# Where a decode kernel turns a group's V sums: behind the first chunk of the next K pair, or behind its first half

## The chip, the cores and the metric

One core of a Trainium2 chip. The metric is device time in microseconds of one execution. The kernel before took 1346.06 us (median of three runs, 1346.02 to 1346.26). All runs below are of state fast, and every verdict compares a kernel with the kernel before, run on the same chip in the same rounds.

## The reference

Two branches are mixed. Branch A, which takes nearly all the time, is attention for one decoded token over a cache: batch 4, 32 heads, 8192 keys of 128 elements, in bf16.

```python
q = (x @ wq).reshape(B, Sq, H, Dh).transpose(0, 2, 1, 3)
scores = jnp.einsum("bhqd,bhkd->bhqk", q, k_cache) * (Dh ** -0.5)
p = _softmax(scores, axis=-1)
o = jnp.einsum("bhqk,bhkd->bhqd", p, v_cache)
a = o.transpose(0, 2, 1, 3).reshape(B, Sq, H * Dh) @ wo
...
return g * a + (1 - g) * b      # b: a gated MLP on the same token, g: a sigmoid gate
```

The K cache and the V cache are 268 MB each and each byte is used once. So the core has to bring in about 0.58 GB whatever it computes.

## The kernel before

K and V come in "pairs" of two ring slots, 4.2 MB a slot, for four heads. The ring has 5 slots (NS) and all loads go out in program order on one queue, that of SP. A load waits until the slots that it writes are free.

```python
    def load_pair(src, n, apart=False):
        a = slots(2)
        if a + 1 < NS and not apart:
            lo = a * RING
            nc.sync.dma_start(out=flat[:, lo:lo + 2 * n], in_=src)     # one load into two slots
            return [flat[:, lo:lo + n], flat[:, lo + n:lo + 2 * n]]
        halves = [ring[:, a], ring[:, (a + 1) % NS]]                   # or one load for each slot
        ...
```

A K pair is worked off in 8 chunks (RD), four (JT) in each slot. DVE transposes a chunk into T, of which there are two buffers, and PE multiplies T with the spread-out query.

```python
    def k_pair(d):
        ...
        ks = load_pair(kv_view(A_k_cache, d), RING)
        for n in range(RD):
            kn, c = ks[n // JT], n % JT
            T = ttp.tile([P, CJ, 2, 32, 2], BF, name="T", tag="T")
            nc.vector.transpose(out=T[:]..., in_=kn[:, c * CJ * Dh:(c + 1) * CJ * Dh]...)       # L370
            ...
            for he in range(4):
                ...
                for z in range(2):
                    nc.tensor.matmul(sps[:, z, :], lhsT=Z[:, he, s:s + P], rhs=T[...], ...)    # L376
            if n == 0:
                flush()
            if n == 2:
                flush_late()
        if t == GD - 1:
            softmax(g)
```

Four pairs make a group. V pairs follow the K pairs at a distance of a group. When a group's last V pair is done, ACT and DVE gather its sums into OS; what then remains to be done (PE turns the sums so that the 128 elements of a head lie along the partitions, and DVE scales them) is only noted down, and `flush()` and `flush_late()` emit it at a later place in PE's and DVE's programs:

```python
        def finish():
            oT = small([P, GH])
            for q in range(4):                                   # the "turning": fp32, four matmuls
                nc.tensor.matmul(oT[:, :], lhsT=o_sb[:, q * Dh:(q + 1) * Dh],                   # L466
                                 rhs=selg[:, q].rearrange("p t s -> p (t s)"), start=(q == 0), stop=(q == 3))

            def scaled():                                        # the scaling, on DVE
                ...
                nc.vector.scalar_tensor_tensor(out=OT[:, hg:hg + GH, b], in0=oT[:, :], ...)     # L471
            late.append(scaled)
        pending.append(finish)
```

The order is K pair d, V pair d - 4, K pair d + 1, and so on. Of eight groups, six are turned in a K pair (pairs 8, 12, 16, 20, 24 and 28), one in a V pair and one at the end of the program.

Of the kernel before, what the change touches and what calls it, by code (L numbers as in the profile page):

```python
# [56 lines left out]
def kernel(  # L57
# [25 lines left out]
    JT = JR // CJ  # L83
# [38 lines left out]
# [5 lines that stand above are left out]
            nc.sync.dma_start(out=flat[:, lo:lo + 2 * n], in_=src)  # L127
            return [flat[:, lo:lo + n], flat[:, lo + n:lo + 2 * n]]
        halves = [ring[:, a], ring[:, (a + 1) % NS]]
        for i, half in enumerate(halves):  # L130
            nc.sync.dma_start(out=half[:, 0:n], in_=src[:, i * n:(i + 1) * n])
        return halves
# [202 lines left out]
    def flush():  # L335
        while pending:
            pending.pop(0)()

    def flush_late():
        while late:  # L340
            late.pop(0)()
# [4 lines left out]
    def kv_view(cache, d):  # L346
        b, h0 = heads(d)
        return cache[b, h0:h0 + NQ].rearrange("h (r j) d -> (h r) (j d)", j=2 * JR)

    def spread(d):  # L350
        b, h0 = heads(d)
        Z = Zt[d % 2]
        nc.gpsimd.tensor_tensor(out=Z[:, :, QP - 1:QP - 1 + P].rearrange("p e (q c) -> p e q c", c=QP)[:, :, :, 0],  # L353
                                in0=qa[:, :, h0:h0 + NQ, b], in1=mq[:].to_broadcast([P, 4, NQ]), op=ALU.mult)

    def k_pair(d):
        g, t = divmod(d, GD)
        Z = Zt[d % 2]
        if d == 0:
            spread(0)  # L360
        if d + 1 < ND:
            spread(d + 1)
        if t == 0:
            S_ps[g] = scp.tile([P, 2, 512], F32, name="S_ps")
        sps = S_ps[g]
# [4 lines that stand above are left out]
            nc.vector.transpose(out=T[:].rearrange("p j h i e -> p (j h i e)").bitcast(U32),  # L370
                                in_=kn[:, c * CJ * Dh:(c + 1) * CJ * Dh].bitcast(U32))
            s = QP - 1 - (RD * t + n)
            for he in range(4):
                half, e = divmod(he, 2)
                for z in range(2):
                    nc.tensor.matmul(sps[:, z, :], lhsT=Z[:, he, s:s + P], rhs=T[:, 16 * z:16 * z + 16, half, :, e],  # L376
                                     start=(t == 0 and n == 0 and he == 0),
                                     stop=(t == GD - 1 and n == RD - 1 and he == 3))
            if n == 0:
                flush()  # L380
            if n == 2:
                flush_late()
        if t == GD - 1:
            softmax(g)
# [102 lines left out]
    for kind, d in order:  # L487
        if kind == "k":
            k_pair(d)
            if d in side:  # L490
                side[d]()
        if (kind, d) == ("v", ND - 1):
            for g in range(2):
                wo_block(g)()
        if kind == "v":
            v_pair(d)
        if (kind, d) == ("k", ND // 2):
            add_x()
        if (kind, d) == ("v", ND - 2):
            o_rows(0, GE)  # L500
# [44 lines left out]
```

## Time and profile before

| what | before |
|---|---|
| time, median of 3 | 1346.06 us |
| moved by the loads | 576.2 MB, 429 GB/s over the span |
| the load queue's share of 16 DMA engines | 99.5% |
| PE busy, DVE busy | 78%, 46% |
| K and V loads in one piece, issue to landing (medians) | 33.3 and 29.8 us |

These are lines of the page of the kernel before: busy time by engine; the share of DMA busy and GB/s in 40 equal slices of the span; the load queue; and the chain of waits that ended last.

```profile
span 1343.2 us, 7989 instructions
...
PE 1050.1 (78%) x4536; PEld 230.3 (17%) x2348; DVE 617.8 (46%) x358; ACT 51.4 (4%) x46; POOL 58.7 (4%) x91
...
DMA  9999999999999999999999999999999999999998
GB/s 414 440 427 431 436 430 425 446 427 424 440 430 427 440 433 422 442 434 428 436 434 433 424 431 436 434 434 439 418 424 437 434 429 434 432 429 442 422 425 335
...
q1 hardware_dynamic: 14132, 575.69, 99.5%
...
DMA 62%; PE 20%; DVE 11%; issue 6%; another core or an unknown queue 0%; DVEq 0%; ACT 0%; SPq 0%
DMA ring<-in_A_k_cache_dram 52%; PE S_ps L376 11%; DVE T L370 11%; PE o_ps L447 8%; DMA ring<-in_A_v_cache_dram 7%; DMA ring<-in_B_w_gate_dram 3%; DMA ring<-in_A_wo_dram 1%; PE small L466 1%; DVEq L370 0%; PE acc L212 0%; ACT OS L459 0%; ACT res L513 0%; SPq L142 0%; SPq L144 0%
```

The digits 9 and the 99.5% say that the DMA engines hardly rest. Packets of one engine can overlap (a share in the windows below reaches 1.10), so the share alone is a sign of it and no proof. The chain needs care. It gives PE 20% and DVE 11%, which looks as if a third of the span were the engines'. But a load of the chain begins with its issue, not with its first byte, so the piece "DVE T" or "PE S_ps" between two loads only says what the second load's issue waited for. Whether that issue was late is not in the chain.

The first K pair of a group, at 482.8 us, shows the place that the change is about. First DVE's timeline (start, duration, instruction, count, and in brackets the idle time before it with what ended it). The eight transpositions of K pair 12 stand in three rows; the scaling L471 is behind the third chunk, and the last row is the next K pair's first one.

```profile
482.83 4.51 DVE L370 STREAM_TRANSPOSE T<-ring 128x2048 uint32<-128x2048 uint32 x2 [2.39 <-DMA ring<-in_A_k_cache_dram]
488.90 2.31 DVE L370 STREAM_TRANSPOSE T<-ring 128x2048 uint32<-128x2048 uint32 x1 [1.56 <-PE S_ps L376]
491.13 0.21 DVE L471 SCALAR_TENSOR_TENSOR OT<-small,sgb,rinv 128x16 bf16<-128x16 f32 x1
493.83 11.09 DVE L370 STREAM_TRANSPOSE T<-ring 128x2048 uint32<-128x2048 uint32 x5 [2.48 <-PE S_ps L376]
521.72 2.31 DVE L370 STREAM_TRANSPOSE T<-ring 128x2048 uint32<-128x2048 uint32 x1 [16.80 <-DMA ring<-in_A_k_cache_dram]
```

DVE rests 1.56 us before chunk 2 and 2.48 us before chunk 3. Both are waits for a T buffer: chunk 2 needs the one that PE's chunk 0 reads, chunk 3 the one that PE's chunk 1 reads. PE's timeline of the same stretch:

```profile
485.29 3.57 PE L376 MATMUL S_ps<-T,Z 128*128 128x512 bf16 x8 [6.36 <-DVE T L370]
488.66 1.72 PE L466 MATMUL small<-selg,OS 128*128 128x16 f32 x8
490.22 5.36 PE L376 MATMUL S_ps<-T,Z 128*128 128x512 bf16 x16
496.20 1.90 PE L376 MATMUL S_ps<-T,Z 128*128 128x512 bf16 x8 [0.62 <-DVE T L370]
```

Chunk 0 (8 matmuls) takes 3.57 us, the turning (8 records, since each fp32 matmul is two) 1.72 us, and then the next 16 matmuls 5.36 us, although a chunk at full speed takes 1.90 us. The columns are busy time with counts for PE, PE's weight loads, DVE, ACT and POOL, then the granted clock, the DMA share and GB/s.

```profile
core 0: us, PE busy (x) PEld busy (x) DVE busy (x) ACT busy (x) POOL busy (x), PEclk, DMA share, GB/s
485.30:488.60 3.30, 3.30 (x8) 0.83 (x5) 2.04 (x1) 0.00 (x0) 0.00 (x0) 0.50 1.10 477
488.60:490.20 1.60, 1.60 (x9) 1.54 (x8) 1.30 (x1) 0.00 (x0) 0.00 (x0) 0.50 0.95 410
490.20:493.50 3.30, 3.30 (x9) 0.68 (x6) 1.15 (x2) 0.00 (x0) 0.00 (x0) 0.50 1.01 437
493.50:497.00 3.50, 2.88 (x13) 0.58 (x6) 3.17 (x2) 0.00 (x0) 0.00 (x0) 0.96 0.91 393
```

PE had waited for the load and started at half clock, and the clock came back only after chunk 1, at about 493.8 us. So what stands between chunk 0 and chunk 1 runs at half speed.

When chunk 3 is done, the first slot is free and SP issues the next K load. SP's timeline:

```profile
472.06 0.33 SPq L127 DMA_DIRECT2D ring<-in_A_v_cache_dram  x1
496.17 0.33 SPq L127 DMA_DIRECT2D ring<-in_A_k_cache_dram  x1
```

### The profile page before, as it was taken

Reading aid. Unit: us, or ns where it says so; the run is one execution under the profiler, and the core shown is the slowest. Engines: PE = TensorE matmul, PEld = TensorE weight load, DVE = VectorE, ACT = ScalarE, POOL = GpSimd, SP = SyncE. Lnnn points to the kernel's source line nnn. Section 1 sums busy time; section 2 is a strip of 40 time slices with the busy share of each in tenths; the row PEclk is TensorE's granted clock in tenths of the full one; section 3 lists DMA queues with packets and bytes.
Section 4 is the critical chain, followed back from the end, with each engine's and each line's share of the span. In section 5 each row is a group of like instructions: output and inputs, shape, how many; then the busy total and the mean of one; then the engine's idle time right before and its main releaser. Section 6 shows DMA issues by size and latency. Waiting matters only on the chain.

```text
span 1343.2 us, 7989 instructions
## 1 busy us (share of the span) xinstructions
PE 1050.1 (78%) x4536; PEld 230.3 (17%) x2348; DVE 617.8 (46%) x358; ACT 51.4 (4%) x46; POOL 58.7 (4%) x91
## 2 busy tenths in 40 slices
PE   2565877788797778778987789797789679877898
PEld 0111111111111111111211121111111112111221
DVE  2455655535445554335455446246555254556000
ACT  0000100001000100001000010001000010000000
POOL 4000100001000100001000010000000010000000
PEclk9777988978998989899888889998899799989899
DMA  9999999999999999999999999999999999999998
GB/s 414 440 427 431 436 430 425 446 427 424 440 430 427 440 433 422 442 434 428 436 434 433 424 431 436 434 434 439 418 424 437 434 429 434 432 429 442 422 425 335
DMA packets 14175, 576.20 MB, mean 429 GB/s; under 512 B 1582, under 2 KB 1590, under 8 KB 2108
## 3 DMA queue, kind: packets, MB, share of 16 engines
q1 hardware_dynamic: 14132, 575.69, 99.5%
q8 instruction: 27, 0.44, 0.1%
q14 instruction: 8, 0.07, 0.0%
q10 hardware_dynamic: 8, 0.00, 0.0%
HBM read 575.68 MB, written 0.01 MB: 429 GB/s over the span
## 4 chain that ended last, share of the span: by engine, by line
DMA 62%; PE 20%; DVE 11%; issue 6%; another core or an unknown queue 0%; DVEq 0%; ACT 0%; SPq 0%
DMA ring<-in_A_k_cache_dram 52%; PE S_ps L376 11%; DVE T L370 11%; PE o_ps L447 8%; DMA ring<-in_A_v_cache_dram 7%; DMA ring<-in_B_w_gate_dram 3%; DMA ring<-in_A_wo_dram 1%; PE small L466 1%; DVEq L370 0%; PE acc L212 0%; ACT OS L459 0%; ACT res L513 0%; SPq L142 0%; SPq L144 0%
## 5 line engine op out<-in xcount | busy, mean ns | idle before, releaser
L370 DVE STREAM_TRANSPOSE T<-ring 128x2048 uint32<-128x2048 uint32 x256 | 570.8, 2282 | 498.5 <-DMA ring<-in_A_k_cache_dram 419.2
L376 PE MATMUL S_ps<-T,Z 128*128 128x512 bf16 x2048 | 538.6, 411 | 220.1 <-DVE T L370 220.1
L447 PE MATMUL o_ps<-ring,PB 128*32 128x512 bf16 x2048 | 457.5, 386 | 35.3 <-DMA ring<-in_A_v_cache_dram 35.3
L376 PEld LDWEIGHTS <-Z 128*128 128x128 bf16 x1024 | 106.4, 104 | 644.6 <-issue 625.0
L447 PEld LDWEIGHTS <-PB 128*32 128x32 bf16 x1024 | 100.4, 98 | 388.8 <-issue 367.6
L401 ACT ACTIVATE PTs<-S_ps,negm 128x1024 bf16<-128x1024 f32 x8 | 8.9, 1114 | 993.9 <-DVE negm L398 993.8
L353 POOL TENSOR_TENSOR Z<-qa,mq 128x16 bf16<-128x16 bf16 x32 | 9.1, 286 | 804.9 <-PE S_ps L376 737.8
L460 DVE SCALAR_TENSOR_TENSOR OS<-o_ps,mE,OS 128x512 f32<-128x512 f32 x8 | 6.0, 751 | 68.2 <-ACT OS L459 68.2
L412 POOL COPY PB<-PT 32x1024 bf16<-32x1024 bf16 x16 | 30.3, 1897 | 26.8 <-DVE rex L414 26.5
L410 ACT COPY PB<-PT 32x1024 bf16<-32x1024 bf16 x16 | 30.6, 1913 | 10.7 <-DVE PT L403 10.6
L309 DVE CAST LT<-small 128x64 bf16<-128x64 f32 x2 | 0.5, 225 | 42.9 <-PE small L307 42.9
L394 POOL PARTITION_ALL_REDUCE gmx<-mex x8 | 3.2, 396 | 342.0 <-DVE mex L391 342.0
L159 PE MATMUL small<-identb,x 6*128 6x6 bf16 x8 | 0.6, 196 | 22.3 <-DMA x<-in_gate_w_dram 22.3
L389 DVE TENSOR_REDUCE m<-S_ps 128x1 f32<-128x1024 f32 x8 | 9.8, 1225 | 15.9 <-PE S_ps L376 15.9
L212 PE MATMUL acc<-ring,LT 128*4 128x512 bf16 x64 | 14.9, 378 | 1.9 <-DMA ring<-in_A_wo_dram 1.2
L420 DVE RECIPROCAL rinv<-tot 128x16 f32<-128x16 f32 x8 | 2.0, 248 | 31.0 <-POOL tot L416 31.0
L403 DVE STREAM_TRANSPOSE PT<-PTs 128x1024 bf16<-128x1024 bf16 x8 | 10.0, 1246 | 12.1 <-ACT PTs L401 12.1
L466 PEld LDWEIGHTS small<-selg,OS 128*128 128x128 f32 x64 | 13.4, 293 | 6.7 <-issue 6.2
L466 PE MATMUL small<-selg,OS 128*128 128x16 f32 x64 | 12.3, 330 | 0.0
L212 PE MATMUL acc<-ring,hT 128*4 128x512 bf16 x56 | 12.2, 379 | 0.0
L459 ACT ACTIVATE OS<-o_ps,mE 128x512 f32<-128x512 f32 x8 | 5.5, 687 | 118.3 <-PE o_ps L447 118.3
L246 PE MATMUL o_ps<-ring,xw 128*4 128x512 bf16 x56 | 5.7, 536 | 5.2 <-DMA ring<-in_B_w_gate_dram 5.2
(71 smaller groups left out, 73.8 us busy)
## 6 DMA issues: line engine op xcount, KB each, us to landing
ring<-in_A_k_cache_dram SPq DMA_DIRECT2D x14, 4096.0 KB
ring<-in_A_v_cache_dram SPq DMA_DIRECT2D x14, 4096.0 KB, 28.8
ring<-in_B_w_gate_dram SPq DMA_DIRECT2D x1, 7168.0 KB, 37.2
ring<-in_B_w_up_dram SPq DMA_DIRECT2D x1, 7168.0 KB, 37.7
ring<-in_B_w_down_dram SPq DMA_DIRECT2D x2, 3584.0 KB, 25.8
ring<-in_A_wo_dram SPq DMA_DIRECT2D x6, 1024.0 KB, 21.0
ring<-in_A_v_cache_dram SPq DMA_DIRECT2D x2, 2048.0 KB, 28.6
ring<-in_A_v_cache_dram SPq DMA_DIRECT2D x4, 1024.0 KB, 24.6
```

What stands on the lines that cost most here:

```text
L212: nc.tensor.matmul(out_ap, lhsT=lhsT, rhs=rhs, start=start, stop=True, skip_group_check=True)
L353: nc.gpsimd.tensor_tensor(out=Z[:, :, QP - 1:QP - 1 + P].rearrange("p e (q c) -> p e q c", c=QP)[:, :, :, 0], in0=qa[:, :, h0:h0 + NQ, b], ...
L370: nc.vector.transpose(out=T[:].rearrange("p j h i e -> p (j h i e)").bitcast(U32), in_=kn[:, c * CJ * Dh:(c + 1) * CJ * Dh].bitcast(U32))
L376: nc.tensor.matmul(sps[:, z, :], lhsT=Z[:, he, s:s + P], rhs=T[:, 16 * z:16 * z + 16, half, :, e], start=(t == 0 and n == 0 and he == 0), ...
L389: nc.vector.tensor_reduce(out=m1[:], in_=sps[:].rearrange("p z n -> p (z n)"), axis=AX.X, op=ALU.max)
L401: nc.scalar.activation(out=PTs[:], in_=sps[:].rearrange("p z n -> p (z n)"), func=ACT.Exp, bias=negm[:, 0:1], scale=scale, accum_out=rs[:, ...
L403: nc.vector.transpose(out=PT[:].rearrange("p j i -> p (j i)"), in_=PTs[:])
L410: nc.scalar.copy(out=Bv[at, :, :, q, :], in_=Pv[at])
L412: nc.gpsimd.tensor_copy(out=Bv[at, :, :, q, :], in_=Pv[at])
L447: nc.tensor.matmul(o_ps[row:row + NM, e, :], lhsT=B_[:, RD * t + c, z, w].rearrange("p e s j -> p (e s j)"), rhs=vn[:, j0 * Dh:(j0 + 4) * ...
L460: nc.vector.scalar_tensor_tensor(out=o_sb[:], in0=o_ps[:, 1, :], scalar=mE[:, 1:2], in1=o_sb[:], op0=ALU.mult, op1=ALU.add)
L466: nc.tensor.matmul(oT[:, :], lhsT=o_sb[:, q * Dh:(q + 1) * Dh], rhs=selg[:, q].rearrange("p t s -> p (t s)"), start=(q == 0), stop=(q == 3))
```

## The change

The intent: to let PE get through the first half of the K pair without the turning, so that the first slot comes free sooner and the next K load is issued sooner. Nothing is added or removed.

```diff
-            if n == 0:
+            if n == JT:
                 flush()
-            if n == 2:
+            if n == JT + 2:
                 flush_late()
```

## The prediction

> **What bounds it now.** The loads. The page gives 576.2 MB over a span of 1343.2 us, 429 GB/s, with the load queue holding 99.5% of the 16 DMA engines' time and a 9 in every slice; PE is busy 78%, DVE 46%. The Trainium skill, "DMA: Bandwidth & Descriptors", section Specifications, gives a fabric ceiling of 435 GB/s; the trace's 429 fits that, and contradicts the 358 GB/s HBM limit in the same table. The chain of waits is 62% DMA. It also names PE S_ps (11%) and DVE T (11%), but these lie between one load's landing and the issue of a later load, which then waits in a full queue: the issue table gives K and V loads 28 to 33 us (medians) from issue to landing, although 8.4 MB at 429 GB/s need only 19.6 us. A typical load is issued some 9 us before the queue reaches it.
>
> **What the change does.** No instruction is added or removed. The four fp32 matmuls that turn V's sums (8 records, 0.9 to 1.5 us of PE in the chain) and the DVE scaling (0.21 us) move from behind chunks 0 and 2 of the K pair to behind chunks 4 and 6. Of 8 groups six are touched (K pairs 8, 12, ..., 28); the seventh flushes inside a V pair and the eighth in the tail, both unchanged. One deferred reciprocal (0.25 us, K pair 4) moves too.
>
> **What it is worth locally.** At a group's first K pair PE starts slow (3.57 us per chunk instead of 1.90) and the turning delays its chunk 1. DVE has two T buffers, so its chunk 3 waits: 2.48 us idle at 493.8 us in the timeline, against 0.58 us in a pair without turning (375.0 us). So chunk 3, and the release of the first ring slot, should come about 1.9 us earlier (estimate: the difference). Behind chunk 4 PE is warm and has 0.3 us to spare per chunk, so the turning costs DVE perhaps 0.5 to 1 us at chunk 7, and the pair ends up to 1 us earlier. The wait for OS (1.4 us of ACT and DVE after the last V matmul) is not moved.
>
> **On the critical path.** Nearly nothing. The slot that chunk 3 frees lets the next K load be issued. In the clearest pair that is at 496.2 us; the V load before it occupies the queue until about 502 (K landed at 482.8, plus 19.6): 6 us in hand, more in other groups. Issuing 1.9 us earlier only lengthens its stay in the queue. If I were wrong and every release counted, six times 1.9 us would be 11 us, 0.8%. The end (last V halves, Wo blocks) is untouched.
>
> **Prediction.** 1346.0 us, 8 in 10 between 1344.0 and 1347.5. Faster by over 2%: 0.01; within 2%: 0.98; slower: 0.01.
>
> **What would show it.** After: DVE's idle before chunk 3 of the pairs near 330, 486, 640, 796, 955 and 1108 us falls from about 2.4 to 0.6 us; the K issue there comes about 1.9 us earlier; its issue-to-landing time grows by as much; landing times and GB/s per slice stay. A small new DVE wait appears at chunk 7. The turning takes about 0.9 us, PE being warm.
>
> **What would make it wrong.** If the queue's rate depends on how many loads stand in it, or DVE's accesses disturb the writes, an earlier issue could move the time by a few us. If the order of loads or ACT work came out otherwise, likewise. If the queue runs dry at group starts in a way that 10 us windows hide, up to 11 us could be gained.

## More of the kernel before

The turning as a group of instructions (count, then busy us and mean ns of one, then the idle time before them):

```profile
L466 PE MATMUL small<-selg,OS 128*128 128x16 f32 x64 | 12.3, 330 | 0.0
```

## The result, and the profile after

| | before | after |
|---|---|---|
| median, us | 1346.04 (4 runs, 1345.92 to 1346.26) | 1345.84 (4 runs, 1344.91 to 1346.06) |
| ratio, after to before | | 0.9997, 95% interval 0.998 to 1.0014 |
| span of the profiled run, us | 1343.2 | 1344.3 |

A ratio is the mean time of one kernel's fast runs over that of the other's fast runs of the same rounds, so it is not quite the ratio of the medians. The change makes no difference that can be measured. The instruction order of ACT, POOL and SP is the same in both kernels; only PE and DVE differ, at the places of the diff.

The page after:

```profile
span 1344.3 us, 7989 instructions
...
PE 1040.5 (77%) x4536; PEld 224.8 (17%) x2348; DVE 618.1 (46%) x358; ACT 51.4 (4%) x46; POOL 58.6 (4%) x91
...
DMA  9999999999999999999999999999999999999997
GB/s 414 439 427 429 439 430 428 442 435 421 442 434 423 431 437 431 437 433 426 433 435 437 433 433 426 428 435 432 430 426 436 433 427 445 432 421 442 422 426 317
...
q1 hardware_dynamic: 14132, 575.69, 99.4%
...
DMA 64%; PE 18%; DVE 11%; issue 7%; DVEq 0%; ACT 0%; SPq 0%
DMA ring<-in_A_k_cache_dram 53%; DVE T L370 11%; PE S_ps L376 9%; PE o_ps L447 8%; DMA ring<-in_A_v_cache_dram 7%; DMA ring<-in_B_w_gate_dram 3%; DMA ring<-in_A_wo_dram 1%; PE o_ps L246 0%; PE acc L246 0%; DVEq L370 0%; PE acc L212 0%; PE small L466 0%; ACT OS L459 0%; ACT res L513 0%; SPq L142 0%
```

The rate is the same 429 GB/s, and the slices move up and down by the same few per cent. The part of the chain put down to PE S_ps fell from 11% to 9% and the DMA's part rose from 52% to 53%: the chain's time was relabelled, not shortened.

DVE's timeline for the same K pair 12:

```profile
483.59 4.50 DVE L370 STREAM_TRANSPOSE T<-ring 128x2048 uint32<-128x2048 uint32 x2 [1.28 <-DMA ring<-in_A_k_cache_dram]
489.66 11.08 DVE L370 STREAM_TRANSPOSE T<-ring 128x2048 uint32<-128x2048 uint32 x5 [1.56 <-PE S_ps L376]
500.67 0.21 DVE L471 SCALAR_TENSOR_TENSOR OT<-small,sgb,rinv 128x16 bf16<-128x16 f32 x1
500.88 2.31 DVE L370 STREAM_TRANSPOSE T<-ring 128x2048 uint32<-128x2048 uint32 x1
522.47 2.31 DVE L370 STREAM_TRANSPOSE T<-ring 128x2048 uint32<-128x2048 uint32 x1 [19.28 <-DMA ring<-in_A_k_cache_dram]
```

Chunks 2 to 6 now run in one piece: the 2.48 us before chunk 3 are gone. The scaling stands behind chunk 6 and chunk 7 follows it at once. PE's timeline:

```profile
486.05 5.53 PE L376 MATMUL S_ps<-T,Z 128*128 128x512 bf16 x16 [5.25 <-DVE T L370]
492.02 1.89 PE L376 MATMUL S_ps<-T,Z 128*128 128x512 bf16 x8 [0.44 <-DVE T L370]
...
498.14 0.96 PE L466 MATMUL small<-selg,OS 128*128 128x16 f32 x8
498.95 3.74 PE L376 MATMUL S_ps<-T,Z 128*128 128x512 bf16 x16
```

The first 16 matmuls take 5.53 us and the clock is back within chunk 1, as two windows of this trace show (columns as above):

```profile
488.60:490.20 1.60, 1.60 (x6) 0.29 (x2) 0.54 (x1) 0.00 (x0) 0.00 (x0) 0.58 0.85 369
490.20:493.50 3.30, 2.86 (x14) 0.58 (x6) 3.30 (x2) 0.00 (x0) 0.00 (x0) 1.00 1.06 457
```

The turning takes 0.96 us instead of 1.72. As a group, over all eight turnings:

```profile
L466 PE MATMUL small<-selg,OS 128*128 128x16 f32 x64 | 7.9, 255 | 0.0
```

SP's timeline:

```profile
494.19 0.33 SPq L127 DMA_DIRECT2D ring<-in_A_k_cache_dram  x1
```

The K load goes out at 494.19 us, 10.60 us after the K pair's first transposition (483.59); before, it was 496.17 - 482.83 = 13.34 us. The next K pair's first transposition comes 522.47 - 483.59 = 38.88 us after this one's, and before it came 521.72 - 482.83, 38.89 us. So the load was issued 2.74 us earlier and arrived at the same time. The six pairs, each read in this way (us after the pair's first transposition; in the trace the first of the two transpositions in a row starts with the row):

| K pair | turning, before / after | next K load issued, before / after | pair's last transposition ends, before / after | next K pair begins, before / after |
|---|---|---|---|---|
| 8 | 1.09 / 0.96 | 11.04 / 10.26 | 19.78 / 19.27 | 38.88 / 38.88 |
| 12 | 1.72 / 0.96 | 13.34 / 10.60 | 22.08 / 19.60 | 38.88 / 38.88 |
| 16 | 1.72 / 0.96 | 13.33 / 10.14 | 22.08 / 19.15 | 41.83 / 41.89 |
| 20 | 1.72 / 0.96 | 13.15 / 10.60 | 21.90 / 19.61 | 29.10 / 29.09 |
| 24 | 1.72 / 0.96 | 13.34 / 10.60 | 22.09 / 19.61 | 39.00 / 38.71 |
| 28 | 1.33 / 0.96 | 11.28 / 10.20 | 20.03 / 19.21 | 38.87 / 38.88 |

(Pair 16 was itself loaded in two halves and began early, so the next one is further off; the load behind pair 20 is split too, and its first half comes earlier.) The issues of the next K load come 13.1 us earlier in sum over the six pairs, the next K pairs begin no earlier (0.2 us in sum). That is the whole result: the gain is real and the queue swallows it.

In two of the six pairs, 8 and 28, the clock came back during the turning (1.09 and 1.33 us), and there the issue moved by 0.8 and 1.1 us only.

### The profile page after: what moved, and what is told of

Read it like the earlier page. It is cut to its first block, busy times and chain, and to the rows that moved or that the text cites. A ratio compares the mean times of both kernels' runs of the same rounds, so it can differ in the third digit from the quotient of the medians.

```text
span 1344.3 us, 7989 instructions
## 1 busy us (share of the span) xinstructions
PE 1040.5 (77%) x4536; PEld 224.8 (17%) x2348; DVE 618.1 (46%) x358; ACT 51.4 (4%) x46; POOL 58.6 (4%) x91
## 2 busy tenths in 40 slices
DMA packets 14175, 576.20 MB, mean 429 GB/s; under 512 B 1582, under 2 KB 1590, under 8 KB 2108
## 4 chain that ended last, share of the span: by engine, by line
DMA 64%; PE 18%; DVE 11%; issue 7%; DVEq 0%; ACT 0%; SPq 0%
DMA ring<-in_A_k_cache_dram 53%; DVE T L370 11%; PE S_ps L376 9%; PE o_ps L447 8%; DMA ring<-in_A_v_cache_dram 7%; DMA ring<-in_B_w_gate_dram 3%; DMA ring<-in_A_wo_dram 1%; PE o_ps L246 0%; PE acc L246 0%; DVEq L370 0%; PE acc L212 0%; PE small L466 0%; ACT OS L459 0%; ACT res L513 0%; SPq L142 0%
## 5 line engine op out<-in xcount | busy, mean ns | idle before, releaser
L376 PE MATMUL S_ps<-T,Z 128*128 128x512 bf16 x2048 | 528.6, 406 | 228.7 <-DVE T L370 228.5
L410 ACT COPY PB<-PT 32x1024 bf16<-32x1024 bf16 x16 | 30.6, 1912 | 10.7 <-DVE PT L403 10.6
L466 PEld LDWEIGHTS small<-selg,OS 128*128 128x128 f32 x64 | 8.2, 191 | 3.8 <-issue 3.6
L466 PE MATMUL small<-selg,OS 128*128 128x16 f32 x64 | 7.9, 255 | 0.0
```

Source lines behind the costliest of these rows:

```text
L410: nc.scalar.copy(out=Bv[at, :, :, q, :], in_=Pv[at])
```

## The experiments

Theory A: a load that goes into a queue that is still full is not sped up by an earlier issue. There is slack between the issue and the moment from which it would count, the old place of the turning eats some of it, and the new place doesn't. Theory B: each release counts, and the change gives back late what it gains early. Theory C: the release never matters, since PE's and DVE's own spare time hides the turning.

### No turning in a K pair at all

```diff
-            if n == 0:
-                flush()
-            if n == 2:
-                flush_late()
```

The following V pair does it then, behind its first eight matmuls, as V pairs always did with what was pending. (The expectation says four; the kernel's counter goes up once for two matmuls, and the trace has eight before the turning.)

> No turning in any K pair: it is left for the V pair that follows (behind its first four matmuls), so the first K pair of a group has no added PE work at all. Theory A (slack: the first ring slot's release has 6 us or more in hand before the load queue runs dry): 1346 us, within 0.2%, with the K load that follows issued about 10.5 us after the landing of the group's first K pair, as after the change. Theory B (the release does count, but the change loses as much later as it gains early): with both the early and the late cost gone from the K pair, faster by up to 6 x 2.2 = 13 us, so 1333 us.

Measured: 1346.56 us (1345.94 to 1348.41) against 1345.53 us for the kernel before (7 runs), ratio 1.0003, interval 0.9985 to 1.002. In the trace the next K load goes out 10.1 to 11.4 us after the pair's start. With the turning's cost gone from the K pair altogether, nothing is gained: theory B's 13 us are not there.

### The turning sixteen times, at both places, and eight times at the old one

The cost in doubt is made large enough to be seen. The result stays correct, as each repetition starts its sum anew.

```diff
-            for q in range(4):
+            for q in [0, 1, 2, 3] * (16 if g < 6 else 1):      # 8 in the third kernel
```

Behind the first chunk, 16 times:

> Turning behind the first chunk as before, but done 16 times over for the six groups that flush in a K pair. One warm turning takes 0.9 us, so about 13 us are added ahead of the release of the first slot. Theory A: the margins of 5.8 to 8.8 us are used up and the rest is lost, 4.6 to 7.6 us in each of five groups (in the sixth the K load that follows is split and only its second half waits): about 1376 us, 1365 to 1385. Theory B (every us of release counts): 6 x 13 = 80 us, 1426 us. Theory C (the release of that slot never matters, the engines' own slack is what hides the turning): 1346 us.

Behind the first half, 16 times:

> The same 16-fold turning at the change's place, behind the first half. Theory A: the first slot is released before it, and the second slot is wanted only by the V load after the next K load, which has about 12 us in hand: 1346 to 1351 us. So the same added work should cost about 30 us less here than behind the first chunk. Theory B: about 1426 us here too, as any delay counts. Theory C: 1346 us.

Behind the first chunk, 8 times:

> Eight-fold turning behind the first chunk: about 6 us added ahead of the first slot's release. Theory A: just about the smallest margin (5.8 us): 1346 to 1349 us, a threshold and not a slope. Theory B: 6 x 6 = 37 us, 1383 us. Theory C: 1346 us.

| | us | ratio to before (1345.53) | expected by A | by B | by C |
|---|---|---|---|---|---|
| 16 times, first chunk | 1473.46 | 1.0939 | 1365 to 1385 | 1426 | 1346 |
| 16 times, first half | 1446.73 | 1.0740 | 1346 to 1351 | 1426 | 1346 |
| 8 times, first chunk | 1389.77 | 1.0319 | 1346 to 1349 | 1383 | 1346 |

Theory C fell: the release can matter very much. But theory A's numbers were all missed, and the eight-fold run by itself would have spoken for B. The traces show two mis-sized terms.

The first is the dose. These are windows of the kernel with 16 turnings behind the first half (columns as above):

```profile
343.00:345.00 2.00, 2.00 (x20) 2.00 (x20) 0.80 (x1) 0.00 (x0) 0.00 (x0) 1.00 1.14 492
345.00:350.00 5.00, 5.00 (x30) 5.00 (x29) 0.00 (x0) 0.00 (x0) 0.00 (x0) 0.59 1.05 449
350.00:355.00 5.00, 5.00 (x25) 5.00 (x25) 0.00 (x0) 0.00 (x0) 0.00 (x0) 0.50 1.03 446
355.00:360.00 5.00, 5.00 (x25) 5.00 (x25) 0.00 (x0) 0.00 (x0) 0.00 (x0) 0.50 1.00 433
```

The turnings begin at full clock, and about 5 us later the granted clock is at half and stays there, although PE and its weight loads are busy 5.00 of 5.00 us. The 128x16 fp32 matmuls don't hold the clock up. Sixteen turnings therefore took 22.5 to 24.9 us here and 24.2 to 27.3 us behind the first chunk, where 16 x 0.9 = 14 us had been reckoned; eight took 10.6 to 13.7 us, not 7.

The second is the slack. Windows of the kernel with 16 turnings behind the first chunk, around its K pair 8, which begins at 327.48 us; its next K load is issued at 366.41 us:

```profile
345.00:355.00 10.00, 10.00 (x49) 10.00 (x48) 0.00 (x0) 0.00 (x0) 0.00 (x0) 0.50 0.01 3
355.00:360.40 5.40, 5.40 (x27) 5.40 (x27) 0.00 (x0) 0.00 (x0) 0.00 (x0) 0.50 0.00 0
360.40:366.40 6.00, 6.00 (x17) 1.16 (x9) 2.56 (x2) 0.00 (x0) 0.00 (x0) 0.52 0.00 0
```

The queue runs dry early in the first of these rows (bytes are counted where their packet starts): in the trace of this run the last packet of the V load ahead ends 18.9 us after the start of the K pair. Then there are 3, 0 and 0 GB/s until the K load is issued. So the loss is visible as an empty queue. After the issue, 0.95 us pass to the first packet (0.95 to 0.97 us in ten such loads of the 16-fold and 8-fold kernels), and the next K pair begins 22.9 to 23.4 us after the issue (pair 20, whose load is split, aside). In the eight-fold kernel it was 21.9 to 23.4 us. A pair that streams in a full queue takes half of 38.88 us, 19.4 us. So a load into an empty queue pays 2.5 to 4 us more than one in a full queue, and the issue has to come that much before the queue is dry.

With the doses as they were, theory A's account closes for the first chunk. The starts of the K pairs that follow the six, less those of before, sum to 125 us with 16 turnings and 40 us with 8; the medians rose by 127.9 and 44.2 us. The packet records say that this is time of an empty queue: if each packet that is missing from 16 in flight, one for each engine, counts as a sixteenth, the time lost between the starts of K pairs 1 and 31 is 124.5 us with 16 turnings and 42.6 us with 8, against 0.5 us in the kernel before and 0.2 us in the kernel after. With 16 turnings behind the first half the next K load is issued at 10.3 to 11.2 us, as early as ever. What is late there is the pair's end, 43 to 45 us after its start: DVE is not free when the next K pair has landed, and the V load for the second slot goes out late (52.4 us after the start of pair 8, 28.3 us in the changed kernel). I had left that out.

So after these four runs the mechanism of A stood, but a line through 1, 8 and 16 turnings didn't look like a threshold. The next three kernels were made to find one.

### Twice and four times, near the threshold

The same edit with 2 and with 4.

Twice behind the first chunk:

> Turning behind the first chunk, done twice. Read from the runs before this: a K load issued when the queue is empty takes 22 to 23 us from issue to its first use, and its predecessors end 38.9 us after the group's first K pair landed, so an issue up to 15.8 to 16.9 us after that landing is free, and a later one loses the excess. A second cold turning (1.7 us) moves the issue from 13.3 to 15.0 us. Hinge theory (A, with the margin set right): still free, 1346 us within 0.2%. Slope theory (each us of the release counts somewhere): 6 x 1.7 = 10 us, 1356 us.

Four times behind the first chunk:

> Turning behind the first chunk, done four times: issue at about 18.4 us after the landing, 2 us past the hinge, in four or five of the groups. Hinge theory: 1352 to 1362 us. Slope theory: 6 x 5.1 = 31 us, 1377 us. If the release never counted: 1346 us.

Four times behind the first half:

> The same four turnings at the change's place. Hinge theory: the first slot's issue stays at 10.6 us, the second slot is freed at about 24 us, and the V load that wants it waits for the V pair before it anyway: free, 1346 us within 0.2%, so 6 to 16 us better than the four turnings behind the first chunk. That would show that what the change buys is margin. Slope theory: as behind the first chunk, 1377 us.

| | us (runs) | ratio to before (1345.88, 11 runs) | 95% interval |
|---|---|---|---|
| 2 times, first chunk | 1347.90 (6) | 1.0010 | 0.9997 to 1.0023 |
| 4 times, first chunk | 1353.88 (6) | 1.0060 | 1.0045 to 1.0074 |
| 4 times, first half | 1347.74 (5) | 1.0009 | 0.9996 to 1.0021 |

The numbers expected by the hinge (a threshold: issues before it are free) were met by all three, within 1346 us plus or minus 0.2%, 1352 to 1362 and 1346 again; those expected by a slope (1356, 1377 and 1377) were not.

K pair 12 with four turnings behind the first chunk, from the timelines of DVE and of SP:

```profile
483.99 4.51 DVE L370 STREAM_TRANSPOSE T<-ring 128x2048 uint32<-128x2048 uint32 x2 [2.83 <-DMA ring<-in_A_k_cache_dram]
500.11 11.28 DVE L370 STREAM_TRANSPOSE T<-ring 128x2048 uint32<-128x2048 uint32 x5 [3.16 <-PE S_ps L376]
524.42 2.31 DVE L370 STREAM_TRANSPOSE T<-ring 128x2048 uint32<-128x2048 uint32 x1 [13.03 <-DMA ring<-in_A_k_cache_dram]
```

```profile
502.45 0.33 SPq L127 DMA_DIRECT2D ring<-in_A_k_cache_dram  x1
```

The load is issued 502.45 - 483.99 = 18.46 us after the start and the next pair begins after 40.43 us: 1.55 us late. With four turnings behind the first half:

```profile
483.82 4.50 DVE L370 STREAM_TRANSPOSE T<-ring 128x2048 uint32<-128x2048 uint32 x2 [1.90 <-DMA ring<-in_A_k_cache_dram]
489.69 11.09 DVE L370 STREAM_TRANSPOSE T<-ring 128x2048 uint32<-128x2048 uint32 x5 [1.36 <-PE S_ps L376]
522.84 4.50 DVE L370 STREAM_TRANSPOSE T<-ring 128x2048 uint32<-128x2048 uint32 x2 [16.93 <-DMA ring<-in_A_k_cache_dram]
```

```profile
494.22 0.33 SPq L127 DMA_DIRECT2D ring<-in_A_k_cache_dram  x1
```

The load is issued after 10.40 us and the next pair begins after 39.02 us. Here the extra turnings delay only chunk 7.

Put together from these traces, each read as in the table of the six pairs, this is the threshold (us after the pair's start):

| kernel, K pair | next K load issued | next K pair begins |
|---|---|---|
| after, 12 | 10.60 | 38.88 |
| before, 12 | 13.34 | 38.88 |
| 2 times, first chunk, 12 | 15.05 | 38.87 |
| 4 times, first chunk, 8 | 15.36 | 38.88 |
| 4 times, first chunk, 12 | 18.46 | 40.43 |
| 8 times, first chunk, 8 | 21.90 | 43.92 |
| 8 times, first chunk, 12 | 25.29 | 48.46 |
| 16 times, first chunk, 12 | 38.94 | 62.08 |

In these rows the issue is free up to 15.4 us, and from 18.5 us on each us is lost in full. Reckoned back from 18.46 and 21.90 us, where the loss is 1.55 and 5.04 us, the line starts at 16.9 us; from the longest one, 38.94 - 23.20, it starts at 15.7 us; over all pairs of the 8-fold and 16-fold kernels but 16 and 20 it starts at 15.5 to 17.1 us. The kernel before, at 13.34 us, stood about 2 to 4 us ahead of it in its worst pairs. The kernel after, at 10.60 us, stands about 5 to 6.5 us ahead.

Two cautions. The table leaves out pair 16, which begins early, and pairs 20 and 24 of the four-fold kernel: in these two, with the load issued at 15.3 us, the next K pairs begin 1.4 and 0.8 us later than before. That isn't laid to the issue here, as the packets missing there make 0.0 and 0.3 us, and a period without a turning (pair 13) is 1.5 us longer in the same trace; single periods are not sure to better than that. And the corner is soft. By the count of missing packets the queue begins to thin out 13 to 14 us after the pair's start (pair 24 of the kernel before: 0.4 us lost), and the whole loss is 0.5 us before, 1.9 us with two turnings and 4.9 us with four behind the first chunk, and 0.2 us after.

The four-fold kernels also price what the change buys: 6 us (1353.88 against 1347.74, with intervals that don't meet), which the kernel as it is does not need. Whether the 2 us of the two-fold kernel and of the four-fold one behind the half are real isn't settled by the times, as both intervals hold 1; their traces lack 1.9 and 1.7 us of packets.

### One chunk later instead of four

```diff
-            if n == 0:
+            if n == 1:
                 flush()              # with four turnings
-            if n == 2:
+            if n == 3:
                 flush_late()
```

> The four turnings behind the second chunk (scaling behind the fourth) instead of the first. DVE's chunk 3 writes the buffer that PE's chunk 1 reads, so work placed behind chunk 1 on PE can't delay chunk 3, and with it the first slot's release. Theory A: the K load is issued at 10.2 to 11.4 us after the landing as with no turning in the pair, and the time is 1346 to 1349 us, as with the four turnings behind the first half, not 1354 us as behind the first chunk: one chunk later is as good as four. If it were PE's total delay in the first half that counts: 1352 to 1356 us.

Measured: 1348.09 us (1346.07 to 1349.28) against 1346.59 us, ratio 1.001, interval 0.9996 to 1.0023. The next K load is issued 10.3 to 11.1 us after the pair's start, in all six pairs. So what delayed the release was not PE's total work in the first half but the work ahead of PE's chunk 1, whose T buffer DVE's chunk 3 needs. Moving the turning by one chunk frees the slot as early as moving it by four.

### A ring of four slots

```diff
-    NS = 5
+    NS = 4
```

This takes the slack away: a K load needs both slots of the K pair before it.

> The kernel before with a ring of 4 slots instead of 5. A K load then needs both slots of the K pair before it, so it can't be issued before that pair's last chunk: 22.1 us after its landing in a group's first pair, about 19.9 us in the others, past the hinge of 16 us in all of them. Expected for both theories: each of 32 periods longer by about 3.5 us, about 1455 us. This is the one against which the next is read.

> The same 4-slot ring with the turning behind the first half. Theory A (the change ends a group's first K pair 2.5 us earlier, by the two traces 19.6 instead of 22.1 us, and only spare time in the queue hides it): with no spare time it shows, up to 6 x 2.5 = 15 us (1.0%) faster than the 4-slot ring with the turning behind the first chunk. If the earlier end is given back elsewhere (theory B): no difference.

Measured: 1447.89 us (4 runs, 1442.57 to 1449.74) with the turning behind the first chunk, ratio 1.0745; 1440.47 us (5 runs, 1438.28 to 1443.82) behind the first half, ratio 1.0698. The base came out near the expected 1455 us: a load is issued 19 to 20 us after the pair's start in every period from pair 4 on, past the threshold, and the next K pair begins after 41 to 43 us.

The comparison of the two places is inconclusive as to the cause. The difference is 7 us (the intervals, 1.0726 to 1.0765 and 1.0683 to 1.0713, don't meet), half of the 15 expected, and its sign is right, but the traces don't show it where it should be. In this kernel the clock comes back earlier: with the turning behind the first chunk it takes 0.96 us in four of the six pairs (1.10 and 1.45 in the others), and the pairs' ends sum to 117.4 us, against 117.7 us behind the first half. The 22.1 us from which I had worked out the gain do not occur. The spans of the two profiled runs are 1440.8 and 1439.6 us. Where the 7 us of the timed runs come from is open. The profiled run with the turning behind the first chunk was the fastest of its four by 4 us; the other three have lower mean clocks (0.882 to 0.885 against 0.890), so their turnings may have met the half clock more often, but they left no trace.

### Half the loads

Every K and V load but those of the last V pair brings the first half of each slot only, and the engines read that half twice. The result is wrong on purpose; the engines' work is the same. The diff is abridged: the loads in two pieces are halved likewise.

```diff
-            nc.sync.dma_start(out=flat[:, lo:lo + 2 * n], in_=src)
+            nc.sync.dma_start(out=ring[:, a:a + 2, 0:n // 2], in_=src.rearrange("p (h n) -> p h n", h=2)[:, :, 0:n // 2])
...
-                                in_=kn[:, c * CJ * Dh:(c + 1) * CJ * Dh].bitcast(U32))
+                                in_=kn[:, c % 2 * CJ * Dh:(c % 2 + 1) * CJ * Dh].bitcast(U32))
...
-                                         rhs=vn[:, j0 * Dh:(j0 + 4) * Dh], ...
+                                         rhs=vn[:, j0 % 64 * Dh:(j0 % 64 + 4) * Dh], ...
```

> Wrong result on purpose: every K and V load brings only the first half of each slot, and the engines read that half twice, so all engine work stays and the loads (290 MB less) no longer bound. Expected about 1100 us, bound by PE and DVE. This is the one against which the next is read.

> The same halved loads (wrong result on purpose) with the turning behind the first half. If the 2.2 us that the change saves at a group's start in the loaded kernel were saved engine time as such, 6 x 2.2 = 13 us (1.2%) faster than with the turning behind the first chunk. If they came from PE's slow clock after a wait for a load (theory A's reading of the traces: chunk 0 takes 3.57 us there, 1.90 us warm), PE stays warm here and the places differ by less than 3 us.

Measured: 1175.13 us behind the first chunk (4 runs, 1174.49 to 1178.00) and 1174.64 us behind the first half (4 runs, 1173.78 to 1175.98); ratios 0.8731 and 0.8724, with intervals that overlap. The base was missed by 75 us. PE was busy 84% of the span; what it waits for in the rest I did not follow up, as the comparison doesn't need it.

Two things follow. The loads do bound the kernel: with 264 MB less (576.20 - 311.96 on the two pages; the expectation had said 290) and all engine work kept, 171 us go away. And the place is worth less than 3 us without the load bound as well, since the turning takes 0.96 to 1.42 us at the old place then and the six pairs end at 19.4 to 20.1 us there, against 19.6 to 19.7 us at the new one.

## Why the prediction was right

**The time.** 1346.0 us was predicted and 1345.84 us measured, in the range of 1344.0 to 1347.5. The loads bound the kernel, as predicted from the page: 429 GB/s before and after, and 171 us less with fewer bytes. The Trainium skill, "DMA: Bandwidth & Descriptors", section Specifications, gives 435 GB/s as the ceiling of the fabric, and both traces agree with a kernel just below it on the mean.

**The mechanism.** "Issuing 1.9 us earlier only lengthens its stay in the queue" was right and is shown: the load was issued 2.74 us earlier in pair 12 and the next pair began at the same 38.88 us. The fear that "the queue runs dry at group starts" was unfounded for this kernel: it is never without a packet in flight there, and by the count of missing packets about 0.5 us was to be gained by filling it better.

**The slack was mis-sized.** The prediction gave "6 us in hand", reckoned to the moment at which the queue would be dry. It left out that a load into an empty queue takes 22 to 23.4 us to use and not 19.4. The measured slack is about 2 to 4 us. The result did not hang on the difference, but it was not far from it: with one more turning of 1.7 us the queue begins to thin out. The Trainium skill, in the same page, section "Latency and other measured facts", gives about 600 ns to the first byte on this path; the runs show 0.95 us from the start of the issue to the first packet, of which the issue instruction takes 0.33 us, so they agree if the page counts from the end of the issue, which it doesn't say. The rest lies in the load's end, by the packet records of ten such loads: the last packet starts 19.0 to 20.3 us after the issue and is in flight for about 2.4 us, and the first transposition follows its end by 0.5 to 0.7 us. In a full queue packets of the next load fill these 2.4 us; an issue that comes too late leaves them empty.

**The local gain was mis-sized, and unevenly so.** 1.9 us was predicted for each of six pairs. It was 2.5 to 3.2 us in four pairs and 0.8 and 1.1 us in two, 2.2 us in the mean. The prediction had taken the 2.48 us of DVE idle of one pair for all six; it said that this idle "falls from about 2.4 to 0.6 us", but it was 2.29 to 2.49 us in four pairs and 0.18 and 0.42 us in pairs 8 and 28 from the start, and it fell to nothing in five pairs and to 0.62 us in one. The cause is the clock. The Trainium skill, "TensorE: Matmul & The Clock Gate", Part 1, says that the clock is at half until the array has been busy for a window of about 3.4 us, and that the windows run freely. The trace shows 0.50 and 1.00, and its stretches at half clock around these pairs are 3.41, 6.83 and 10.24 us long, multiples of 3.41. In the kernel before they are 6.83 us in pairs 8 and 28, where the clock came back during the turning, and 10.24 us in the four others, where it came back only around the end of the following chunk. So the same instruction order cost 1 us or 3 us.

**No cost at the new place.** "Perhaps 0.5 to 1 us at chunk 7" did not appear: chunk 7 follows the scaling at once, and the pair ends 2.3 to 2.9 us earlier in four pairs rather than "up to 1 us". The turning took 0.96 us there, where 0.9 was predicted.

**A misreading.** The prediction said that 429 GB/s contradicts the 358 GB/s of the same table. The page's section Bandwidth says that its own single-core measurements (of loads issued from GpSimd), up to 425 GB/s, hold while the other core of the pair is idle, and that 358 GB/s is the share when both stream. One core runs here, and 429 agrees with that.

## What to carry to other kernels

Before moving work to make a buffer come free sooner, find out when the transfer's issue begins to count: read the issue against the moment at which the queue ahead runs dry, less what a load into an empty queue takes longer. Here an issue up to about 15 us after the pair's start cost next to nothing, so 13 us of earlier issues bought nothing but margin, and the four-fold turning showed that margin to be worth 6 us in a kernel that needs it. To find such a threshold, grade the dose finely (2, 4, 8 times), for a single large one looked like a slope; and check in the trace that the dose was what you meant it to be. Where the packet records can be read, count those in flight: here the kernel before had 0.5 us to gain.

## What the Trainium skill lacked or had wrong

- "TensorE: Matmul & The Clock Gate", section "Why this matters for your kernels", says to avoid idle gaps of more than about 3 us to keep the clock. The runs show a fall without any gap: during repeated fp32 matmuls of 128x16, with PE and its weight loads busy 5.00 of 5.00 us, the granted clock went from 1.00 to 0.50 within about 5 us and stayed there for the 15 us that followed. A turning took 1.7 us then instead of 0.96. (The profile models the ends of matmuls, so gaps inside can't be excluded; whether the small shape or the fp32 does it, no run tells apart.)
- The same page has the cost of a cold start, but not that small matmuls in the middle of it can put the recovery off: in pair 12 the clock was back about 11 us after the pair's start with a turning behind chunk 0 (at 493.8 us) and about 6.3 us after it without (in the kernel after, the windows give 0.58 from 488.6 to 490.2 us and 1.00 from 490.2 on). Over the six pairs it was 10.4 to 11.6 us in four and 6.1 and 6.6 us in two with the turning, and 5.1 to 8.4 us in the kernel after and the one without a turning.
- "DMA: Bandwidth & Descriptors", section "Anatomy of one DMA", gives a fixed cost of about 2 us for one load of the other path. For this path, behind an empty queue, an 8.4 MB load took 21.9 to 23.4 us from issue to first use against 19.4 us in a stream, so 2.5 to 4 us more; no page has the number that one needs for slack.
- The same page, section "Where 436 GB/s comes from", says that for HBM to SBUF the HBM side (about 358 GB/s) binds. With one core running, this kernel moved 429 GB/s over 1343 us, as the page's own 425 GB/s lets one expect.
